# Decode attention with an MLP beside it: TensorE's attention work as one loop of four passes, with separate buffers for K and V

## The chip, the cores and the metric

The kernel runs on one core of a Trainium2 chip. The metric is the device time of one execution in microseconds (us), as the median of several runs. Times inside an execution come from one profiled run and are counted from the start of its span. TensorE is written PE, VectorE DVE, ScalarE ACT, GpSimd POOL, and SyncE, which issues nearly all DMAs here, SP. The core's DMA work is spread over 16 DMA engines.

## The reference

One token `x` of 1024 elements is normalised. Branch A is attention over a long cache: 32 query heads, 4 KV heads (8 query heads share one), 65,536 cached positions of 128 elements. Branch B is a small MLP with two residual steps. The weights and the two caches are bfloat16; K and V are 64 MiB each, and everything that is read is 169.87 MB.

```python
x = A_x; xn = layernorm(x)
# A: q = xn @ wq; for each of 4 KV heads, 8 query heads:
scores = einsum("bhqd,bhkd->bhqk", q, k) * Dh ** -0.5
o = einsum("bhqk,bhkd->bhqd", softmax(scores), v)
a = o.reshape(1, 1, 4096) @ wo
# B, on xn: h = gelu(layernorm(xn) @ w1) is shifted along the sequence
# and multiplied by w2; with one token every shifted part is zero, so x1 = xn
b = x1 + gelu(layernorm(x1) @ w3) @ w4
out = x + a + b
```

## The kernel before, in words

**Prologue.** `wq` (8 MiB), `w1`, `w2` (2 MiB each) and `w3` (7 MiB) are read into a large tile `KV` of three slots, 64 KiB in each partition, 8 MiB in all per slot. q is computed and spread into the tile `Yall` (L369), and branch B is computed up to the vector `gh_bf`, which is later multiplied by `w4`.

**Attention.** The cache is worked through in 8 blocks m (two for each KV head h) of 32,768 positions; the K part and the V part of a block are one slot each (8 MiB, one DMA of 128 rows of 64 KiB). A load i is K of block (i-3)/2 for odd i and V for even i. Slots rotate: `slot(i)` is i mod 3 (L278). So K and V share three buffers. `issue(i)` (L281) puts a load on SP's queue, where it waits until the slot's last readers and writers are done. V of block m+1 is issued after `QK(n+3)` of block m (L584), since its slot is the one that held K of block m; K of block m+2 is issued after the last `PV` of block m (L605), since its slot held V of block m. The first loads and the last stand outside this pattern: K of block 0 is issued behind the q projection, V of block 0 behind the use of `w2`, K of block 1 behind the end of the prologue; `wo` takes the place of the load behind the last K, and `w4` follows in four pieces (L532).

A block has four sub-blocks n to n+3, and their work is written out by hand in one order for all engines (L557 to L605). Each engine executes its own part of this order, in order. The pieces:

- `Ttr` (L436): DVE transposes K in place, 32x32 blocks, as float32 pairs of bfloat16. A sub-block takes four instructions of 128x1024. They are interleaved with the small DVE steps below: the pieces of sub-block n+2 and n+3 stand between `MAX`, `EXP` and `PTr`.
- `QK` (L448): 16 matmuls against `Yall` of the head, into the PSUM bank `S_ps[n % 4]`.
- `MAX` (L455 to L458): a maximum over two banks on DVE, a small product `Rm` on DVE, a matmul on PE that brings the groups together in `M_ps`.
- `EXP` (L465 to L476): on DVE the running minimum `brun` of the negated maxima; on ACT the exponentials `p_sb` of two sub-blocks with their sums; the factor `ff` by which older sums are scaled.
- `PT` and `PTr` (L479, L483): a permuting matmul into the one bank `PT_ps`, then a DVE transpose into `pT_f`.
- `PV` (L492): 16 matmuls of `pT_f` with V into `OT_ps`.
- `FLUSH` (L500 to L505): two sub-blocks' result is added to `O_acc`; at a head's first, ACT copies it.
- `combine_1` and `combine_2` (L509 to L527): a head's sum is inverted, and its four rows of output are brought into the columns of `o_bf`. For head h-1 they stand in the first block of head h, behind `QK(n)` and behind `QK(n+1)`; for the last head behind the loop.

**Output.** `out_resid` (L552), the 32 rows of `o_bf` times `wo`, and the 28 rows of `gh_bf` times `w4` (L543) accumulate in one PSUM bank; a copy (L612) and a DMA (L613) bring the result out.

**Synchronisation.** A small planner in Python records for each engine a list of waits and operations. Each engine has one semaphore that counts its finished operations (`_Q`, `c_pe`, `c_dve`, ...), each DMA channel another. For each buffer `_deps` (L73) adds a wait for each semaphore that wrote or reads it, unless the same engine has waited for as high a value of that semaphore before. PE also waits on its own semaphore. PE's whole program, prologue, eight blocks and output, is written out as straight code of some 3,340 records in the trace (1,627 weight loads, 1,611 matmuls, 98 semaphore instructions and a drain).

The order of one block before:

```python
Ttr(n, range(4)); QK(n)
Ttr(n + 1, range(4)); QK(n + 1)
Ttr(n + 2, [0, 1]); MAX(2 * m); Ttr(n + 2, [2]); EXP(2 * m); Ttr(n + 2, [3])
QK(n + 2); PT(n); Ttr(n + 3, [0]); PTr(n)
PT(n + 1); Ttr(n + 3, [1]); PTr(n + 1); Ttr(n + 3, [2, 3])
PV(n); QK(n + 3); issue(6 + 2 * m)
PV(n + 1); MAX(2 * m + 1); EXP(2 * m + 1); FLUSH(2 * m)
PT(n + 2); PTr(n + 2); PT(n + 3); PTr(n + 3)
PV(n + 2); PV(n + 3); FLUSH(2 * m + 1); issue(7 + 2 * m)
```

Of the kernel before, what the change touches and what calls it, by code (L numbers as in the profile page):

```python
# [13 lines left out]
class _Q:  # L14
    def __init__(self, name, sem):
        self.name = name
        self.sem = sem
        self.ops = []
        self.cnt = 0
        self.waited = {}  # L20

    def wait(self, ev):
        if ev is None:
            return
        sem, val = ev
        if self.waited.get(sem, 0) >= val:
            return
        self.waited[sem] = val
        self.ops.append((0, sem, val))

    def op(self, fn, tick=True):
        if tick:
            self.cnt += 1
            self.ops.append((1, fn, True))
            return (self.sem, self.cnt)
        self.ops.append((1, fn, False))
        return None

    def dma(self, fn, sem, val):
        self.ops.append((2, fn, sem))  # L40
        return (sem, val)

    def emit(self, eng):
        for o in self.ops:
            if o[0] == 0:
                eng.wait_ge(o[1], o[2])
            elif o[0] == 1:
                ins = o[1](eng)
                if o[2]:
                    ins.then_inc(self.sem, 1)  # L50
            else:
                o[1](eng).then_inc(o[2], 16)
# [20 lines left out]
def _deps(q, reads, writes):  # L73
    for b in reads:
        for s, v in b.w.items():
            q.wait((s, v))
    for b in writes:
        for s, v in b.w.items():
            q.wait((s, v))
        for s, v in b.r.items():  # L80
            q.wait((s, v))
# [12 lines left out]
def _op(q, fn, reads=(), writes=(), partial=False):  # L94
    _deps(q, reads, writes)
    ev = q.op(fn, True)
    _done(ev, reads, writes, partial)
    return ev
# [25 lines left out]
def bass_parallel_sum__gqa_block_cached__mixer_s_mlp__decode_kernel(  # L124
# [31 lines left out]
    with ExitStack() as es:  # L156
# [18 lines left out]
        Yall = sb("Yall", [P, HKV, 4, 4, G], BF)  # L175
        p_sb = sb("p_sb", [P, 2, 512], BF)
# [64 lines left out]

        q_pe = _Q("pe", sem("c_pe"))
        q_dve = _Q("dve", sem("c_dve"))
        q_act = _Q("act", sem("c_act"))
# [10 lines left out]
        b_x = _B(); b_xT = _B(); b_xn = _B(); b_xn2 = _B(); b_qT = _B(); b_Y = _B()  # L255
        b_ln = _B(); b_misc = _B(); b_h1 = _B(); b_x1 = _B(); b_xn3 = _B(); b_gh = _B(); b_acc = _B()
        b_KV = [[_B() for _ in range(16)] for _ in range(3)]
# [4 lines left out]
        b_Oacc = _B(); b_L = _B(); b_cb = _B(); b_o = _B(); b_orow = _B()  # L262
# [9 lines left out]
        b_w1 = b_KV[1][0:4]  # L272
        b_w2 = b_KV[1][4:8]
# [4 lines left out]
        def slot(i):  # L278
            return i % 3

        def issue(i):  # L281
            if i < 3 + 2 * NBLK:
                m, isv = divmod(i - 3, 2)
                h, nb = divmod(m, BPH)
                cache = A_v_cache if isv else A_k_cache
                src = cache[0, h, nb * BLK:(nb + 1) * BLK, :].rearrange("(p c) d -> p (c d)", p=P)
                kv_load(slot(i), "s%d" % slot(i), src, SLOT)
# [5 lines left out]
        q_pool.wait(evs[-1])  # L293
# [7 lines left out]
        q_pool.wait(ev)  # L301
# [7 lines left out]
        q_pool.wait(ev)  # L309
# [114 lines left out]
        for q in (q_pe, q_dve, q_act, q_pool):  # L424
            q_sp.wait((q.sem, q.cnt))
# [5 lines left out]
        def Ttr(n, idx):  # L431
            m, sub = divmod(n, 4)
            s = slot(3 + 2 * m)
            for ix in idx:
                o = 4096 * sub + 1024 * ix
                _op(q_dve, lambda e, o=o: e.transpose(out=KV32[:, s, o:o + 1024], in_=KV32[:, s, o:o + 1024]),  # L436
                    reads=[b_KV[s][4 * sub + ix]], writes=[b_KV[s][4 * sub + ix]])

        def QK(n):
            m, sub = divmod(n, 4)  # L440
            h = m // BPH
            s = slot(3 + 2 * m)
            fns = []
            for we in range(4):
                w_hi, e_ = divmod(we, 2)
                for cm in range(4):
                    mv = bass.AP(KV[:].tensor, s * SLOT + sub * 8192 + cm * 128 + w_hi * 64 + e_, [[kvstep, P], [512, 16], [2, 32]])
                    fns.append(lambda e, we=we, cm=cm, mv=mv: e.matmul(  # L448
                        S_ps[32 * cm:32 * cm + 32, n % 4, :], Yall[:, h, we, :, :].rearrange("p a g -> p (a g)"), mv,
                        start=(we == 0), stop=(we == 3), tile_position=(0, 32 * cm)))  # L450
            _grp(q_pe, fns, reads=b_KV[s][4 * sub:4 * sub + 4] + [b_Y], writes=[b_S[n % 4]])

        def MAX(g):
# [3 lines left out]
                reads=[b_mrow[k], b_const], writes=[b_R[k]])  # L457
# [3 lines left out]
        def EXP(g):  # L461
# [4 lines left out]
            else:  # L466
# [5 lines left out]
                reads=b_S[2 * k:2 * k + 2] + [b_brun[k]], writes=b_p + [b_lp[k]])  # L472
# [9 lines left out]
        def PTr(n):  # L482
            _op(q_dve, lambda e: e.transpose(out=pT_f[:, n % 2, :], in_=PT_ps[:, :]), reads=[b_PT], writes=[b_pT[n % 2]])  # L483

        def PV(n):
# [9 lines left out]
            _grp(q_pe, fns, reads=[b_pT[n % 2]] + b_KV[s][4 * sub:4 * sub + 4], writes=[b_OT[g % 2]], partial=(last == 1))  # L495

        def FLUSH(g):
            k = g % 2
            if g % (2 * BPH) == 0:
                _op(q_act, lambda e: e.activation(O_acc[:, 0:512], OT_ps[:, k, :], ACTF.Copy), reads=[b_OT[k]], writes=[b_Oacc])  # L500
                _op(q_dve, lambda e: e.tensor_copy(O_acc[:, 512:513], lp[:, k:k + 1]), reads=[b_lp[k]], writes=[b_L])
                return
            _op(q_dve, lambda e: e.scalar_tensor_tensor(out=O_acc[:, 512:513], in0=O_acc[:, 512:513], scalar=ff[:, k:k + 1], in1=lp[:, k:k + 1], op0=ALU.mult, op1=ALU.add),
                reads=[b_ff[k], b_lp[k], b_L], writes=[b_L])
            _op(q_dve, lambda e: e.scalar_tensor_tensor(out=O_acc[:, 0:512], in0=O_acc[:, 0:512], scalar=ff[:, k:k + 1], in1=OT_ps[:, k, :], op0=ALU.mult, op1=ALU.add),  # L505
                reads=[b_ff[k], b_OT[k], b_Oacc], writes=[b_Oacc])

        def combine_1(h):
            _op(q_pe, lambda e: e.matmul(M_ps[:, 32:33], Dmat_f[:, :], O_acc[:, 512:513], start=True, stop=True),  # L509
                reads=[b_L, b_const], writes=[b_M])  # L510
            _op(q_dve, lambda e: e.reciprocal(cb_rL[:, :], M_ps[:, 32:33]), reads=[b_M], writes=[b_cb])
            _op(q_dve, lambda e: e.tensor_scalar(out=cb_W[:, :, :, :].rearrange("p t g i -> p (t g) i"),
                                                 in0=maskT[:, :, :].rearrange("p t g -> p (t g)").unsqueeze(2).broadcast_to([P, 4 * G, 4]), scalar1=cb_rL[:, 0:1], scalar2=None, op0=ALU.mult),
                reads=[b_cb, b_const], writes=[b_cb])

        def combine_2(h):
            r0 = 32 * h
            fns = []
            for t in range(4):
                fns.append(lambda e, t=t: e.matmul(M_ps[r0:r0 + 32, 128:256], cb_W[:, t, :, :].rearrange("p g i -> p (g i)"), O_acc[:, t * P:(t + 1) * P],  # L520
                                                   start=(t == 0), stop=(t == 3), tile_position=(0, r0)))
            _grp(q_pe, fns, reads=[b_Oacc, b_cb], writes=[b_M])
            _op(q_dve, lambda e: e.tensor_tensor(out=cb_R[r0:r0 + 32, :].rearrange("p (a j) -> p a j", j=32), in0=M_ps[r0:r0 + 32, 128:256].rearrange("p (a j) -> p a j", j=32),  # L523
                                                 in1=maskD[r0:r0 + 32, :].unsqueeze(2).broadcast_to([32, 4, 32]), op=ALU.mult),
                reads=[b_M, b_const], writes=[b_cb])
            _op(q_dve, lambda e: e.reduce_sum(cb_o[r0:r0 + 32, :], cb_R[r0:r0 + 32, :].rearrange("p (a j) -> p j a", j=32), axis=AX.X), reads=[b_cb], writes=[b_cb])
            _op(q_dve, lambda e: e.tensor_copy(o_bf[r0:r0 + 32, :], cb_o[r0:r0 + 32, :]), reads=[b_cb], writes=[b_o], partial=True)  # L527
# [4 lines left out]
        def w4_dma(i):  # L532
            r0, nr = w4_parts[i]
            _dma(q_sp, chan("w4%d" % i), lambda e: e.dma_start(out=KV[:, slot(20), r0 * D:(r0 + nr) * D], in_=rows_src(B_w4, r0, nr)), writes=[b_W4[i]])
# [21 lines left out]

        for m in range(NBLK):  # L557
            n = 4 * m
            h, nb = divmod(m, BPH)
            comb = nb == 0 and h > 0  # L560
            Ttr(n, range(4))
            QK(n)
            if comb:
                combine_1(h - 1)
            Ttr(n + 1, range(4))
            QK(n + 1)
            if comb:
                combine_2(h - 1)
            Ttr(n + 2, [0, 1])
            MAX(2 * m)  # L570
            Ttr(n + 2, [2])
            EXP(2 * m)
            Ttr(n + 2, [3])
            QK(n + 2)
            PT(n)
            Ttr(n + 3, [0])
            PTr(n)
            PT(n + 1)
            Ttr(n + 3, [1])
            PTr(n + 1)  # L580
            Ttr(n + 3, [2, 3])
            PV(n)
            QK(n + 3)
            issue(6 + 2 * m)  # L584
            if m == NBLK - 1:
                for i in range(len(w4_parts)):
                    for bk in b_KV[slot(20)]:
# [13 lines left out]
            FLUSH(2 * m + 1)  # L601
            if m == NBLK - 2:
                kv_load(slot(19), "s%d" % slot(19), A_wo.rearrange("(p r) n -> p (r n)", p=P), SLOT)
            else:
                issue(7 + 2 * m)  # L605
        out_resid()
        combine_1(HKV - 1)
        combine_2(HKV - 1)
        out_rows([(o_bf[:, j:j + 1], KV[:, slot(19), j * D:(j + 1) * D]) for j in range(32)], b_KV[slot(19)] + [b_o])
        for i, (r0, nr) in enumerate(w4_parts):  # L610
            out_rows([(gh_bf[:, r:r + 1], KV[:, slot(20), r * D:(r + 1) * D]) for r in range(r0, r0 + nr)], [b_W4[i], b_gh], last=(i == len(w4_parts) - 1))
        _op(q_dve, lambda e: e.tensor_copy(orow[:, :], OUT), reads=[b_OUT], writes=[b_orow])  # L612
        ev_out = _dma(q_sp, chan("out"), lambda e: e.dma_start(out=out[0, 0, :].rearrange("(j n) -> j n", j=4), in_=orow[0:97:32, :]), reads=[b_orow])  # L613
        q_sp.wait(ev_out)
# [13 lines left out]
        q_pe.emit(nc.tensor)  # L628
# [28 lines left out]
```

## Time and profile before

| what | value |
|---|---|
| median of 8 runs | 402.06 us (401.66 to 402.37) |
| the profiled execution's own time | 402.11 us |
| its span, first to last instruction | 400.9 us |
| read from HBM | 169.87 MB, 424 GB/s over the span |
| PE, DVE, ACT, POOL busy | 178.6, 224.6, 25.2, 7.1 us |
| granted TensorE clock, mean | 0.623 |
| loads of K issued (block 2, 3, 4) | 105.83, 142.75, 188.12 us |
| loads of V issued (block 1, 2, 3) | 96.44, 133.27, 179.37 us |
| first transpose of block 0, 1, 2, 3 | 71.7, 108.14, 146.89, 188.7 us |

The span is the time from the first to the last instruction that the profiler recorded; the execution's own time is 1.2 us longer. The page divides the span into 40 slices and gives for each the busy tenths of every engine and the DMA engines' mean share. A timeline lists an engine's instructions with start, duration, and in square brackets the idle time before one and what released it. An answer by stages gives for stretches of time the busy time of each engine, the granted PE clock, and, as the last two columns, the share of 16 DMA engines and the rate of the packets that began in that stretch; a packet of 64 KiB counts with its whole duration in the stretch in which it begins, so short stretches can show more than 1.

### The profile page before, as it was taken

Reading aid. Unit: us, or ns where it says so; the run is one execution under the profiler, and the core shown is the slowest. Engines: PE = TensorE matmul, PEld = TensorE weight load, DVE = VectorE, ACT = ScalarE, POOL = GpSimd, SP = SyncE. Lnnn points to the kernel's source line nnn. Section 1 sums busy time; section 2 is a strip of 40 time slices with the busy share of each in tenths; the row PEclk is TensorE's granted clock in tenths of the full one; section 3 lists DMA queues with packets and bytes.
Section 4 is the critical chain, followed back from the end, with each engine's and each line's share of the span. In section 5 each row is a group of like instructions: output and inputs, shape, how many; then the busy total and the mean of one; then the engine's idle time right before and its main releaser. Section 6 shows DMA issues by size and latency. Waiting matters only on the chain.

```text
span 400.9 us, 3966 instructions
## 1 busy us (share of the span) xinstructions
PE 178.6 (45%) x1611; PEld 71.3 (18%) x1627; DVE 224.6 (56%) x347; ACT 25.2 (6%) x53; POOL 7.1 (2%) x30
## 2 busy tenths in 40 slices
PE   0035669136434523374345242633462345437655
PEld 0022435011111101121111020111121111102332
DVE  0024230985498446764985548659746684696400
ACT  1000000011001100101011001000110011010100
POOL 5000000000000000000000000000000000000000
PEclk9998656555655565658556655575576655555785
DMA  9999999999999999999999999999999999999994
GB/s 419 419 391 486 387 465 451 425 420 425 425 425 459 445 425 425 414 445 426 453 438 425 414 419 451 433 439 438 414 432 419 452 438 427 432 440 432 395 419 192
DMA packets 3770, 170.13 MB, mean 424 GB/s; under 512 B 548, under 2 KB 552, under 8 KB 808
## 3 DMA queue, kind: packets, MB, share of 16 engines
q1 hardware_dynamic: 3608, 169.87, 98.4%
q8 instruction: 13, 0.21, 0.2%
q14 instruction: 5, 0.04, 0.0%
q10 hardware_dynamic: 144, 0.00, 0.0%
HBM read 169.87 MB, written 0.00 MB: 424 GB/s over the span
## 4 chain that ended last, share of the span: by engine, by line
DMA 41%; DVE 30%; PE 24%; issue 3%; another core or an unknown queue 2%; POOL 0%; SPq 0%; ACT 0%; DVEq 0%
DMA KV<-in_A_k_cache_dram 28%; DVE KV L436 21%; PE S_ps L448 8%; DMA KV<-in_B_w_dram 7%; DMA KV<-in_A_x_dram 6%; PE OT_ps L492 5%; PE S_ps L385 3%; DVE pT_f L483 2%; PE M_ps L400 2%; PE S_ps L353 2%; DVE mrow L455 2%; PE M_ps L520 1%; DVE Yall L369 1%; PE PT_ps L479 1%
## 5 line engine op out<-in xcount | busy, mean ns | idle before, releaser
L436 DVE STREAM_TRANSPOSE KV<-KV 128x1024 f32<-128x1024 f32 x128 | 148.6, 1211 | 7.5 <-DMA KV<-in_A_k_cache_dram 7.4
L448 PE MATMUL S_ps<-KV,Yall 128*32 128x512 bf16 x512 | 60.7, 622 | 113.1 <-DVE KV L436 113.1
L492 PE MATMUL OT_ps<-KV,pT_f 128*32 128x512 bf16 x512 | 58.4, 605 | 1.3 <-PE OT_ps L492 1.3
L448 PEld LDWEIGHTS S_ps<-KV,Yall 128*32 128x32 bf16 x512 | 16.7, 125 | 145.8 <-DVE KV L436 129.9
L483 DVE STREAM_TRANSPOSE pT_f<-PT_ps 128x512 f32<-128x512 f32 x32 | 22.6, 706 | 28.3 <-PE S_ps L448 12.0
L470 ACT ACTIVATE p_sb<-S_ps,brun 128x1024 bf16<-128x1024 f32 x16 | 17.8, 1113 | 279.4 <-DVE brun L468 174.7
L455 DVE TENSOR_REDUCE mrow<-S_ps 128x1 f32<-128x1024 f32 x16 | 19.5, 1216 | 16.8 <-PE S_ps L448 16.7
L479 PE MATMUL PT_ps<-p_sb,permR 128*128 128x512 bf16 x16 | 9.0, 560 | 37.2 <-DVE pT_f L483 37.2
L492 PEld LDWEIGHTS OT_ps<-KV,pT_f 128*32 128x32 bf16 x512 | 17.0, 131 | 34.9 <-issue 33.1
L505 DVE SCALAR_TENSOR_TENSOR O_acc<-O_acc,ff,OT_ps 128x512 f32<-128x512 f32 x12 | 8.9, 746 | 22.4 <-PE OT_ps L492 22.4
L385 PE MATMUL S_ps<-KV 128*32 128x512 bf16 x88 | 12.5, 569 | 2.9 <-DVE KV L333 2.9
L458 PE MATMUL M_ps<-Rm,Lmat 128*128 128x16 bf16 x16 | 3.1, 192 | 22.3 <-DVE Rm L456 22.3
L313 DVE CAST KV<-KV 128x8 f32<-128x8 bf16 x1 | 0.2, 172 | 22.3 <-DMA KV<-in_A_x_dram 22.3
L479 PEld LDWEIGHTS PT_ps<-p_sb,permR 128*128 128x128 bf16 x32 | 3.3, 102 | 43.1 <-ACT p_sb L470 15.4
L612 DVE CAST orow<-S_ps 128x256 bf16<-128x256 f32 x1 | 0.4, 424 | 16.9 <-PE S_ps L543 16.9
L400 PE MATMUL M_ps<-ident_f,pT_f 64*128 64x2 f32 (+2 forms) x32 | 7.9, 373 | 2.3 <-DVE pT_f L393 2.3
L400 PEld LDWEIGHTS M_ps<-ident_f,pT_f 64*128 64x128 f32 (+2 forms) x32 | 7.7, 326 | 4.7 <-DVE pT_f L393 4.7
L393 DVE COPY pT_f<-S_ps 64x512 f32<-64x512 f32 (+1 forms) x3 | 2.1, 686 | 11.4 <-PE S_ps L385 11.4
L543 PE MATMUL S_ps<-KV,gh_bf 128*1 128x256 bf16 x112 | 5.6, 362 | 5.8 <-DMA KV<-in_B_w_dram 5.6
L523 DVE TENSOR_TENSOR cb_R<-M_ps,maskD 32x128 f32<-32x128 f32 x4 | 1.2, 288 | 12.1 <-PE M_ps L520 12.1
L458 PEld LDWEIGHTS M_ps<-Rm,Lmat 128*128 128x128 bf16 x16 | 1.6, 102 | 34.5 <-DVE Rm L456 34.5
L338 PE MATMUL M_ps<-KV 8*128 8x8 bf16 x1 | 0.2, 161 | 16.2 <-DVE Dmat_f L337 16.2
(82 smaller groups left out, 97.3 us busy)
## 6 DMA issues: line engine op xcount, KB each, us to landing
KV<-in_B_w_dram SPq DMA_DIRECT2D x1, 7168.0 KB, 48.0
KV<-in_B_w_dram SPq DMA_DIRECT2D x1, 4352.0 KB, 21.6
KV<-in_B_w_dram SPq DMA_DIRECT2D x2, 2048.0 KB, 28.3
KV<-in_B_w_dram SPq DMA_DIRECT2D x1, 1792.0 KB, 25.6
KV<-in_B_w_dram SPq DMA_DIRECT2D x1, 768.0 KB, 27.0
KV<-in_B_w_dram SPq DMA_DIRECT2D x1, 256.0 KB, 27.2
KV<-in_A_k_cache_dram SPq DMA_DIRECT2D x8, 38.8
KV<-in_A_v_cache_dram SPq DMA_DIRECT2D x8, 30.1
```

Source lines behind the costliest of these rows:

```text
L353: fns.append(lambda e, j=j, b=b, jj=jj: e.matmul(S_ps[32 * jj:32 * jj + 32, b, :], xn_bf[:, j:j + 1].broadcast_to([P, 32]), KV[:, 0, j * H ...
L385: fns.append(lambda e, j=j, k=k, mv=mv: e.matmul(S_ps[32 * (k % 4):32 * (k % 4) + 32, bank + k // 4, :], vec[:, j:j + 1].broadcast_to([P, ...
L400: fns.append(lambda e, b=b, nb=nb, c=c: e.matmul(M_ps[:, c0 + 16 * b + c:c0 + 16 * b + 4 * nb:4], pT_f[0:32 * nb, b, c:512:4], ident_f[0:3 ...
L436: _op(q_dve, lambda e, o=o: e.transpose(out=KV32[:, s, o:o + 1024], in_=KV32[:, s, o:o + 1024]), reads=[b_KV[s][4 * sub + ix]], writes=[b_ ...
L448: fns.append(lambda e, we=we, cm=cm, mv=mv: e.matmul(S_ps[32 * cm:32 * cm + 32, n % 4, :], Yall[:, h, we, :, :].rearrange("p a g -> p (a g ...
L455: _op(q_dve, lambda e: e.reduce_max(mrow[:, k:k + 1], S_ps[:, 2 * k:2 * k + 2, :].rearrange("p b c -> p (b c)"), axis=AX.X), reads=b_S[2 * ...
L470: _op(q_act, lambda e: e.activation(p_sb[:, :, :].rearrange("p b c -> p (b c)"), S_ps[:, 2 * k:2 * k + 2, :].rearrange("p b c -> p (b c)") ...
L479: _op(q_pe, lambda e: e.matmul(PT_ps[:, :], permR[:, :], p_sb[:, n % 2, :], start=True, stop=True), reads=[b_p[n % 2], b_const], writes=[b ...
L483: _op(q_dve, lambda e: e.transpose(out=pT_f[:, n % 2, :], in_=PT_ps[:, :]), reads=[b_PT], writes=[b_pT[n % 2]])
L492: fns.append(lambda e, q=q, q4=q4: e.matmul(OT_ps[32 * q4:32 * q4 + 32, g % 2, :], pT_bf[:, n % 2, q, :, 1], KV[:, s, 8192 * sub + 512 * q ...
L505: _op(q_dve, lambda e: e.scalar_tensor_tensor(out=O_acc[:, 0:512], in0=O_acc[:, 0:512], scalar=ff[:, k:k + 1], in1=OT_ps[:, k, :], op0=ALU ...
L543: fns.append(lambda e, lhs=lhs, rhs=rhs, jj=jj: e.matmul(S_ps[32 * jj:32 * jj + 1, 0, 0:256], lhs, rhs[:, 256 * jj:256 * jj + 256], start= ...
```

## The change

PE's program for the eight blocks becomes one loop of four passes, a pass for each head (two blocks). With it come:

- Two new semaphores, `l_dve` and `l_act`, count those DVE and ACT operations that PE waits for, from zero in each pass. All loads of V use one channel, `v`. At the end of a pass PE waits until these three have reached the pass's total and subtracts it, then branches back.
- K is in slot 0 and slot 2 by turns, V always in slot 1. V of block m+1 can so be issued only after the last `PV` of block m: `issue(6 + 2 * m)` moves from behind `QK(n+3)` to behind `FLUSH(2m+1)`, directly ahead of `issue(7 + 2 * m)`. The `w4` loads stay behind `QK(n+3)` of the last block, into slot 2; `wo` goes into slot 0.
- `QK` reads a tile `Ycur`, into which DVE copies the head's part of `Yall` at the start of each pass (`YC`).
- A `Ttr` is one DVE instruction of 128x4096 in place of four of 128x1024, and is no longer interleaved with `MAX`, `EXP` and `PTr`: `Ttr(n+2)` stands whole ahead of `MAX`, `Ttr(n+3)` whole behind `PTr(n+1)`.
- `combine` stands in one piece at the end of its own head, ahead of the branch, and its matmuls write the partitions 0 to 31 of `M_ps`.
- A head's first `FLUSH` copies `O_acc` on DVE, not ACT; the other `FLUSH` does its large step first.
- The planner keeps for each event what was known when it was issued, and leaves out a wait that another wait implies; PE no longer waits on its own semaphore.

The new block (the diff of the loop, cut):

```diff
 def slot(i):
-    return i % 3
+    m, isv = divmod(i - 3, 2)
+    return 1 if isv else 2 * (m % 2)
...
-    comb = nb == 0 and h > 0
-    Ttr(n, range(4))
+    if nb == 0:
+        loop_sync(h)
+        q_pe.mark({q.loop_sem: q.count[q.loop_sem] for q in (q_dve, q_act)})
+        YC(h)
+    Ttr(n)
     QK(n)
-    if comb:
-        combine_1(h - 1)
-    Ttr(n + 1, range(4))
+    Ttr(n + 1)
     QK(n + 1)
-    if comb:
-        combine_2(h - 1)
-    Ttr(n + 2, [0, 1])
+    Ttr(n + 2)
     MAX(2 * m)
-    Ttr(n + 2, [2])
     EXP(2 * m)
-    Ttr(n + 2, [3])
     QK(n + 2)
     PT(n)
-    Ttr(n + 3, [0])
     PTr(n)
     PT(n + 1)
-    Ttr(n + 3, [1])
     PTr(n + 1)
-    Ttr(n + 3, [2, 3])
+    Ttr(n + 3)
     PV(n)
     QK(n + 3)
-    issue(6 + 2 * m)
...
     PV(n + 2)
     PV(n + 3)
     FLUSH(2 * m + 1)
+    issue(6 + 2 * m)
     if m == NBLK - 2:
-        kv_load(slot(19), "s%d" % slot(19), A_wo.rearrange("(p r) n -> p (r n)", p=P), SLOT)
+        kv_load(0, "wo", A_wo.rearrange("(p r) n -> p (r n)", p=P), SLOT)
     else:
         issue(7 + 2 * m)
+    if nb == BPH - 1:
+        combine(h)
```

The pieces that are called, and how PE's program is written out:

```diff
+def YC(h):
+    _op(q_dve, lambda e: e.tensor_copy(Ycur[:, :, :, :].rearrange("p w a g -> p (w a g)"), Yall[:, h, :, :, :].rearrange("p w a g -> p (w a g)")),
+        reads=[b_Y], writes=[b_Yc], loop=True)
...
+def Ttr(n):
+    m, sub = divmod(n, 4)
+    s = slot(3 + 2 * m)
+    o = 4096 * sub
+    _op(q_dve, lambda e: e.transpose(out=KV32[:, s, o:o + 4096], in_=KV32[:, s, o:o + 4096]), reads=[b_KV[s][sub]], writes=[b_KV[s][sub]], loop=True)
...
-q_pe.emit(nc.tensor)
+q_pe.emit(nc.tensor, q_pe.ops[:marks[0]])
+for s_, v in entry.items():
+    nc.tensor.wait_ge(s_, v)
+with nc.tensor.Fori(0, HKV):
+    for waits, o in zip(steps, work[0]):
+        for s_, v in waits.items():
+            nc.tensor.wait_ge(s_, v)
+        q_pe.emit(nc.tensor, [o])
+    for s_, v in totals.items():
+        nc.tensor.wait_ge(s_, v).then_inc(s_, -v)
+q_pe.emit(nc.tensor, q_pe.ops[marks[-1]:])
```

## The prediction, as put on record before the result

> **What bounds the kernel now.** I read the page's slices and DMA queues first. The DMA engines are busy in every slice but the last, and the data queue fills 98.4% of them: 169.87 MB is what the reference must read, so only idle DMA time, or DMA time spent on something else, can be won or lost.
>
> ```profile
> DMA  9999999999999999999999999999999999999994
> q1 hardware_dynamic: 3608, 169.87, 98.4%
> q8 instruction: 13, 0.21, 0.2%
> DMA 41%; DVE 30%; PE 24%; issue 3%; another core or an unknown queue 2%; POOL 0%; SPq 0%; ACT 0%; DVEq 0%
> L436 DVE STREAM_TRANSPOSE KV<-KV 128x1024 f32<-128x1024 f32 x128 | 148.6, 1211 | 7.5 <-DMA KV<-in_A_k_cache_dram 7.4
> ```
>
> The chain (fourth line) ends in DMA or passes through DVE and PE, but this is one chain of several that are equally long: where it runs through DVE, the queue of loads is still full. Next SP's timeline, with each load's issue, and DVE's, with the wait for K of block 2:
>
> ```profile
> 96.44 0.33 SPq L265 DMA_DIRECT2D KV<-in_A_v_cache_dram  x1
> 105.83 0.33 SPq L265 DMA_DIRECT2D KV<-in_A_k_cache_dram  x1
> 133.27 0.33 SPq L265 DMA_DIRECT2D KV<-in_A_v_cache_dram  x1
> 142.75 0.33 SPq L265 DMA_DIRECT2D KV<-in_A_k_cache_dram  x1
> ...
> 146.89 2.37 DVE L436 STREAM_TRANSPOSE KV<-KV 128x1024 f32<-128x1024 f32 x2 [3.45 <-DMA KV<-in_A_k_cache_dram]
> ```
>
> V of block 2, issued at 133.27, is in the queue 13.6 us before K of block 2 has landed (146.89). That lead keeps the engines fed. Last, the stages at both ends (last two columns: DMA share and rate of packets that began there):
>
> ```profile
> 0.50:1.00 0.50, 0.00 (x0) 0.00 (x0) 0.00 (x0) 0.10 (x1) 0.09 (x1) 1.00 0.00 0
> 1.00:1.50 0.50, 0.00 (x0) 0.00 (x0) 0.00 (x0) 0.50 (x1) 0.50 (x5) 1.00 5.08 1704
> ...
> 394.00:395.00 1.00, 0.00 (x0) 0.00 (x0) 0.00 (x0) 0.00 (x0) 0.00 (x0) 0.50 0.69 279
> 395.00:396.00 1.00, 0.59 (x13) 0.38 (x17) 0.00 (x0) 0.00 (x0) 0.00 (x0) 0.50 0.62 236
> 396.00:397.00 1.00, 1.00 (x20) 0.41 (x12) 0.00 (x0) 0.00 (x0) 0.00 (x0) 0.50 0.31 123
> 397.00:398.00 1.00, 0.76 (x16) 0.24 (x12) 0.00 (x0) 0.00 (x0) 0.00 (x0) 0.50 0.09 33
> ```
>
> An idle engine starts 1.0 to 1.6 us after an issue. At the end the share fades over 3 us: the 16 engines don't finish together. The trace's landing records give each engine's share of a load: K of block 1 lands between 106.20 and 108.12, the last piece of `w4` between 394.40 and 397.92. A 64 KB packet takes 2.42 us, eight of them per engine and load 19.37 us, a pair of loads 38.74 us. The spread comes from packets that aren't data: each of the 13 instruction packets of the page occupies one engine for 1.02 to 1.11 us (13 times 1.0 is the page's 0.2%), and the data packet beside it takes 2.9 us, so that engine is 1.55 us later for good. They come each time PE has executed some 256 instructions (3,337 records, 13 packets). The latest engine, with two such delays and small ones, is 3.5 us behind the earliest, and it sets the end: 397.92 to 400.9 is the last rows, the copy and the output DMA, 3.0 us.
>
> **The change, part by part.**
>
> *Length of a block, from its first transpose to its last `PV`, call it L.* Before, blocks without a combine (0, 1, 3, 5, 7) take 34.1, 34.6, 33.7, 33.8, 33.6: mean 34.0; K is transposed at +22.8 (108.14 to 130.94). A merged `Ttr` isn't in the trace. Four pieces take 4.62 (ceiling); one piece of 1.20 plus 3072 elements at the slope between L483 (512 elements, 0.71) and L436 (1024, 1.21), 0.97 ns, is 4.18 (floor); I take 4.4. The new order: three `Ttr` 13.2; `MAX` and `Rm` 1.4 (to 14.6); from `Rm`'s start to the minimum 0.56, `brun` 0.2, ACT 0.33 later (15.5). PE does `QK(n+2)` behind the small matmul, at 15.0; 2.47 from there to `PTr` as in block 1, 1.49 to the next, 0.7 its length: 19.65. The last `Ttr` ends at 24.05. So what the interleaving hid, waits of DVE for PE and ACT, is now open, against shorter transposes: +1.25 (0.4 to 2.1 by the two ends). L is 35.25. PE's waits on itself (0.17 us ahead of four groups in a block at most) give back some 0.25: 35.0. `YC` costs 0.2 (a small copy, L413, takes 0.19); `FLUSH` on DVE 0.75 beside ACT's exponentials; both small.
>
> *Combine.* It no longer stops DVE twice inside the next block (blocks 2 and 4 took 41.2 and 41.6, 7 us more than the others), but stands between heads: `FLUSH` 1.0, sum matmul 0.6, reciprocal and weights 0.5, four float32 products 1.9, three DVE steps 0.9, with handovers 5.1 us, with `YC` 5.3 from the last `PV` to the next transpose. Within a head that gap is 1.0. A head costs 2 x 35.0 + 6.3 = 76.3 against 77.5 of pure DMA: it fits, barely.
>
> *V's single buffer.* V of block m+1 now comes at the end of block m. Block 0 starts at 71.9 (the prologue stays) and ends at 107.0. Before, V of block 1 was issued at 96.44 and its packets began as K of block 1 left the engines, from 106. Now the engines run dry: restart 1.0 to 1.6 after 107.0, and first packets in an empty system took 2.7 to 3.4, not 2.42 (the first loads: all done by 4.3 us after issue). That is as if all began at 107.0 + 1.9 = 108.9. The earliest engine loses 2.8 us, the latest (108.12) only 0.8. Later blocks start with K's landing, so their end, 35.0 later, leaves 3.7 us until the next K, against 1.9 for a restart; behind a combine 2 us less, and early engines may wait, but not the latest. The second buffer for K costs nothing.
>
> *The end.* `wo` and `w4` are issued in the old order behind V of block 7, two loads ahead of need. Block 7 starts with its K (before, at 344.6, behind a late block 6; after, near 346), so its last `PV` and the last combine are over by 386, its rows with `wo` (5.3 us before) by 392; the first piece of `w4` landed at 391.06 before and moves with the DMA time to about 394. Covered. The waits left out on DVE, ACT and SP are semaphore instructions on engines that idle: nothing.
>
> *PE's loop.* Wait and decrement at the pass's end find their counts reached: nothing. The body is some 583 records (3,337 less 439 ahead of the attention and 565 behind it, by four), 2.3 pages of 256. No jump is in this trace. Either the pages are kept (nothing more is fetched), or a jump fetches some again, up to the whole program once more (1,590 instructions, 6 to 7 pages on as many engines) at each of three jumps. PE's own wait is covered: its part of the combine ends about 4.3 us behind the last `PV`, the next `QK` is due at 9.7, and another 2.3 may pass before `MAX` is late; so 7.7 us. The nearest row is straight code: a page for 256 instructions, two delays on the latest engine behind 108. I take that.
>
> [...]
>
> *Sum, for the latest engine.* 108.9 + 288.2 (earliest engine, 106.20 to 394.40) + 2 x 1.55 = 400.2; plus 3.0 of tail, 403.2 of span, against 400.9; plus 1.2 outside the span (402.11 less 400.9), **404.4 us**. The profiled run stands 0.05 above the median.
>
> **The rivals.**
>
> 1. *Forecast, 0.45:* block 0's gap, page delays as before. One to three delays and L within 1 us: 402.7 to 406.5.
> 2. *Each jump brings in much of the program again, 0.20:* three more delays on the same engines: 404.4 + 4.65 = 409.1; with two pages doubled, 407. For it: packets come in whole pages, ahead of use. Against it: nothing shows how many pages are kept.
> 3. *The block's length decides, 0.13:* if L exceeds 36 us or a jump takes over 8 us, a head costs more than 78.5, and the engines wait in every head. At L = 37 it is 80.3: 3 heads x 2.8 above 77.5, 8 us less the 3.1 of page delays that then lie in the waits: 409. For it: the spare of 1.2 us; against it: before, L varied by 1 us only.
> 4. *Fewer pages, 0.20, the other side:* if the loop's pages stay in PE's instruction memory, they are fetched once. With the gap and one delay 402.9, with none 401.3; if block 0 also ends by 105 (L = 33.2) only one delay is left on the earliest engines: 394.4 + 1.55 + 3.0 + 1.2 = 400.2. It turns to faster below one delay, or where the gap is under 1 us.
> 5. *The code isn't reached or the loop costs nothing and nothing else changes, 0.02:* 402.
>
> **How the numbers follow.** 0.2% of 402.06 is 0.8 us, about what can be told from no change here. Faster (under 401.3): 0.12, from rival 4. Same: 0.12, from rivals 4 and 5 and the lower edge of the forecast. Slower: 0.76. The range, 401.0 to 409.5, leaves out a tenth on each side; the forecast's own is 402.7 to 406.5.
>
> **What would show it.** In the changed profile: SP's timeline with V of block 1 issued near 107, and a DMA share of nearly 0 for 1 to 2 us behind 106; no such hole later. `Ttr` with a mean of 4.2 to 4.6. DVE idle inside blocks, at `PTr`. The page's instruction packets: 13 for the forecast, over 25 for rival 2, under 9 for rival 4. Last `PV` to next transpose 5.3 between heads. I am wrong if holes in the DMA share come in every head, if L is off by more than 1 us, or if PE is late at a pass's first `QK`.

## The result and the profile after

The changed kernel takes 404.33 us (median of 14 runs, 401.75 to 406.28); the kernel before takes 402.00 us beside it (40 runs, 401.66 to 402.54). The ratio is 1.0056, 95% interval 1.0045 to 1.0068: slower, as forecast, and within 0.1 us of the forecast time. (Ratios here and below are of the means of the runs, without the profiled one, so they differ a little from the quotient of the medians.) The runs also lie further apart: over 4.5 us, where those of before lie within 0.9. The profiled execution took 404.85 us, with a span of 403.6.

The page of the kernel after has these lines against those of before: the DMA share, the data and the instruction queue, the chain, the transposes.

```profile
DMA  9999999999999999999999999999999999999994
q1 hardware_dynamic: 3608, 169.87, 98.3%
q8 instruction: 6, 0.10, 0.1%
DMA 55%; DVE 25%; PE 17%; issue 1%; another core or an unknown queue 1%; SPq 0%; POOL 0%; ACT 0%
L460 DVE STREAM_TRANSPOSE KV<-KV 128x4096 f32<-128x4096 f32 x32 | 140.0, 4412 | 13.5 <-DMA KV<-in_A_k_cache_dram 13.5
```

The first two lines hardly moved, and that is the trap of this profile: the same 3,608 data packets fill 98.3% of a span that is 2.7 us longer. A packet counts as busy for its whole duration, so engines that work slowly look as busy as before (behind 106, below: share 1.29 against 0.99 for the same 426 GB/s). The third line is a gain: 6 instruction packets where there were 13. In the fourth line the chain runs through DMA for 55% of the span (41% before), and the last shows DVE waiting for K more than before (13.5 us against 7.5).

SP's timeline around block 0's end, and DVE's wait behind it:

```profile
104.01 0.33 SPq L290 DMA_DIRECT2D KV<-in_A_v_cache_dram  x1
104.38 0.43 SPq L290 DMA_DIRECT2D KV<-in_A_k_cache_dram  x1
...
108.17 4.45 DVE L460 STREAM_TRANSPOSE KV<-KV 128x4096 f32<-128x4096 f32 x1 [3.19 <-DMA KV<-in_A_k_cache_dram]
```

V of block 1 is issued only 4.2 us before K of block 1 has landed on all engines; before, it was 11.7 us (96.44 to 108.14). The landing and packet records of the trace, engine by engine, show what that does. Per block: when V of the next block is issued, when the first engine is done with K, the lead between the two, and how long V then takes on the latest engine (from K's last landing to V's last), where 19.37 us is the undisturbed time:

| end of block | V issued | K done, first engine | lead | V on the latest engine |
|---|---|---|---|---|
| 0 | 104.01 | 106.21 | 2.2 | 19.37 + 0.92 |
| 1 | 142.81 | 145.49 | 2.7 | 19.37 + 0.00 |
| 2 | 182.00 | 184.20 | 2.2 | 19.37 + 0.60 |
| 3 | 221.18 | 223.37 | 2.2 | 19.37 + 0.58 |
| 4 | 260.50 | 262.69 | 2.2 | 19.37 + 0.10 |
| 5 | 299.81 | 301.85 | 2.0 | 19.37 + 0.21 |
| 6 | 339.07 | 341.25 | 2.2 | 19.37 + 0.44 |

The sum is 2.85 us. The engines hardly stand idle (some 11 engine-us in all up to 394, of some 6,200); V's first packets are slow, on some engines the second ones, 2.7 to 4.1 us where a packet takes 2.42. Without those of the very first load, 63 packets take over 0.3 us too long up to 380 us, and together they lose 44 engine-us; before it was 16 packets, ten of them directly behind an instruction packet. By stages behind block 0's end (last two columns: DMA share and GB/s of the packets begun there), first after, then before:

```profile
106.00:108.00 2.00, 0.00 (x0) 0.00 (x0) 0.00 (x0) 0.00 (x0) 0.00 (x0) 0.68 1.29 426
108.00:110.00 2.00, 0.00 (x0) 0.00 (x0) 1.83 (x1) 0.00 (x0) 0.00 (x0) 0.50 0.85 328
```

```profile
106.00:108.00 2.00, 0.00 (x0) 0.00 (x0) 0.52 (x1) 0.00 (x0) 0.00 (x0) 1.00 0.99 426
108.00:110.00 2.00, 0.00 (x0) 0.00 (x0) 1.86 (x2) 0.00 (x0) 0.00 (x0) 0.72 1.14 492
```

After the change as many packets begin in the first stage, but they last longer (share 1.29 against 0.99), and fewer follow. The latest engine's sum is 108.15 + 288.2 (what the earliest engine took before, from 106.20 to 394.40) + 2.85 + some 1.5 for an instruction packet in the tail = 400.7; the last landing was at 400.86. That packet begins at 386.92, takes 0.99, and the data packet behind it takes 1.80 in place of 1.29. Before, the last landing was at 397.92.

The loop itself costs PE nothing that shows. DVE's and PE's timeline behind the first branch back:

```profile
147.83 8.76 DVE L460 STREAM_TRANSPOSE KV<-KV 128x4096 f32<-128x4096 f32 x2
...
152.32 0.14 PEld L474 LDWEIGHTS S_ps<-KV,Ycur 128*32 128x32 bf16 x8 [5.88 <-DVE KV L460]
152.32 1.90 PE L474 MATMUL S_ps<-KV,Ycur 128*32 128x512 bf16 x16 [5.43 <-DVE KV L460]
```

The second pass's first `QK` starts about 0.1 us behind its transpose, and what it waited for was DVE, not its own instructions. Instruction packets (the page's q8, 16 KB each) came at 43.6, 79.2, 106.0 and 145.7, then none until 386.9: the second to fourth pass fetched nothing. At the start of the third and the fourth pass the first `QK` also begins 0.1 us behind its transpose (at 230.81 and 309.45).

### The profile page after: what moved, and what is told of

It reads as the page before. It is cut to its first block, busy times and chain, and to the rows that moved or that the text cites. A ratio compares the mean times of both kernels' runs of the same rounds, so it can differ in the third digit from the quotient of the medians.

```text
span 403.6 us, 3656 instructions
## 1 busy us (share of the span) xinstructions
PE 178.7 (44%) x1611; PEld 68.0 (17%) x1627; DVE 222.8 (55%) x259; ACT 23.3 (6%) x49; POOL 7.1 (2%) x30
## 3 DMA queue, kind: packets, MB, share of 16 engines
q1 hardware_dynamic: 3608, 169.87, 98.3%
## 4 chain that ended last, share of the span: by engine, by line
DMA 55%; DVE 25%; PE 17%; issue 1%; another core or an unknown queue 1%; SPq 0%; POOL 0%; ACT 0%
DMA KV<-in_A_k_cache_dram 42%; DVE KV L460 17%; DMA KV<-in_B_w_dram 8%; DMA KV<-in_A_x_dram 5%; PE S_ps L474 4%; PE OT_ps L518 4%; PE S_ps L411 3%; DVE pT_f L509 2%; PE M_ps L426 2%; PE S_ps L379 1%; DVE mrow L481 1%; PE PT_ps L505 1%; DVE Yall L395 1%; DVE pT_f L419 1%
## 5 line engine op out<-in xcount | busy, mean ns | idle before, releaser
L460 DVE STREAM_TRANSPOSE KV<-KV 128x4096 f32<-128x4096 f32 x32 | 140.0, 4412 | 13.5 <-DMA KV<-in_A_k_cache_dram 13.5
L474 PE MATMUL S_ps<-KV,Ycur 128*32 128x512 bf16 x512 | 60.7, 623 | 95.3 <-DVE KV L460 95.3
L474 PEld LDWEIGHTS S_ps<-KV,Ycur 128*32 128x32 bf16 x512 | 14.3, 125 | 132.1 <-DVE KV L460 114.5
L543 PE MATMUL M_ps<-O_acc,cb_W 128*32 128x128 f32 x32 | 6.9, 386 | 2.3 <-DVE cb_W L538 2.3
```

The source lines that it names most:

```text
L460: _op(q_dve, lambda e: e.transpose(out=KV32[:, s, o:o + 4096], in_=KV32[:, s, o:o + 4096]), reads=[b_KV[s][sub]], writes=[b_KV[s][sub]], l ...
L474: fns.append(lambda e, we=we, cm=cm, mv=mv: e.matmul(S_ps[32 * cm:32 * cm + 32, n % 4, :], Ycur[:, we, :, :].rearrange("p a g -> p (a g)") ...
L543: fns.append(lambda e, t=t: e.matmul(M_ps[0:32, 128:256], cb_W[:, t, :, :].rearrange("p g i -> p (g i)"), O_acc[:, t * P:(t + 1) * P], sta ...
```

## The experiments

Two groups were run, each beside the kernel before on the same chip (402.03 us for e1 to e4, 402.13 for e5 to e7). Theory A is that V's late issue makes its first packets slow; B blames the branch and the waits around it; C the longer blocks. A lead is, as above, the time from V's issue to the first engine's landing of the K before it.

| kernel | us (range; runs) | ratio to before, interval | instruction packets | slow packets |
|---|---|---|---|---|
| before | 402.00 (401.66 to 402.54; 40) | 1 | 13 | 16 |
| changed | 404.33 (401.75 to 406.28; 14) | 1.0056 (1.0045 to 1.0068) | 6 | 63 |
| e1 no branch | 404.89 (403.53 to 406.53; 4) | 1.0081 (1.0051 to 1.0110) | 13 | 47 |
| e2 V in halves | 401.17 (400.97 to 401.45; 11) | 0.9979 (0.9970 to 0.9988) | 6 | 6 |
| e3 halves, no branch | 402.55 (402.37 to 403.22; 11) | 1.0014 (1.0005 to 1.0023) | 13 | 12 |
| e4 V and K later | 406.43 (403.89 to 407.32; 4) | 1.0088 (1.0060 to 1.0116) | 6 | 83 |
| e5 V as 3/4 and 1/4 | 401.27 (401.05 to 401.61; 10) | 0.9980 (0.9970 to 0.9989) | 6 | 9 |
| e6 K apart from V | 403.30 (401.96 to 404.92; 10) | 1.0025 (1.0008 to 1.0043) | 6 | 67 |
| e7 before, whole transposes | 403.08 (402.26 to 403.87; 10) | 1.0020 (1.0010 to 1.0029) | 13 | 20 |

Instruction packets are those of the trace's records for the queue q8, taken as PE's (13 with PE's straight code, 6 with the loop, 13 again in e1), one or two of which can lie behind the span's end; slow packets are those of 16 KB and more that took over 0.3 us longer than their size takes undisturbed, up to 380 us, without those of the very first load.

**e1: the changed kernel without the branch.**

```diff
-with nc.tensor.Fori(0, HKV):
+for _ in range(HKV):
```

The body stands four times in PE's program; waits and decrements stay.

> Theory A (V is issued too late: some 2.2 us ahead of the first engine's end of K, so that the first packets of V are slow in nearly every block; the loop itself saves instruction packets): the slow packets stay, the instruction packets come back to about 13, so 405 to 407 us. Rival B (the branch back and the waits at the end of a pass cost the time): without them about 402 us. Rival C (longer blocks from whole transposes): nothing changes, 404.3.

404.89, no faster than with the branch: B, which had about 402, falls. The instruction packets are back, in the page's third part:

```profile
q8 instruction: 13, 0.21, 0.2%
```

The time is just under the 405 to 407 that A gave, and from the changed kernel's 404.33 the four runs can't be told apart. That part of an instruction packet's delay is lost here in the early engines' wait for V is a guess that no run tests; e3, with 12 slow packets in place of 47, shows its cost better.

**e2: V in two halves, the first one issued earlier.**

```diff
+for hf in halves:
+    lo, hi = hf * SLOT // 2, (hf + 1) * SLOT // 2
+    _dma(q_sp, chan("v%d" % hf), ... out=KV[:, 1, lo:hi], in_=src[:, lo:hi], writes=b_KV[1][2 * hf:2 * hf + 2])
...
 PV(n + 1)
+issue(6 + 2 * m, (0,))
...
 FLUSH(2 * m + 1)
-issue(6 + 2 * m)
+issue(6 + 2 * m, (1,))
```

> The loop stays; V is loaded in two halves with a semaphore each, and the first half is issued behind the block's second PV, some 8 us earlier. Theory A: no packet of V takes over 2.6 us, instruction packets stay at 6, so 400.5 to 402.0 us and all runs within 1 us of each other (now 401.75 to 406.28). Rival B: the branch is still there, 404 us. Rival C: the blocks are as long as before, 404 us.

401.17, 0.21% under the kernel before, and all eleven runs within 0.5 us. The order of the work, the single buffer for V, the loop and the whole transposes are those of the changed kernel, and the blocks are about as long (34.1 us on average, 34.2 in the changed kernel, each from the first transpose to the last `PV`); half a load comes earlier, and V's packets are of 32 KB. (e5 speaks of the size.) SP's timeline at block 0's end (the first line is both halves, issued at 98.41 and 105.29; the duration is from the first to the end of the second):

```profile
98.41 7.21 SPq L316 DMA_DIRECT2D KV<-in_A_v_cache_dram  x2
105.66 0.43 SPq L290 DMA_DIRECT2D KV<-in_A_k_cache_dram  x1
```

The lead is 8.0 us (first engine done with K at 106.40), and 6 slow packets are left, of which 4 stand directly behind an instruction packet. Against C this is the plain test: blocks as long as in the changed kernel, and the loss is gone. The halves cost a little: a pair of loads takes the first engine 38.81 us (145.20 to 184.01) where it took 38.72 in the kernel before (144.92 to 183.64), 0.7 us over eight blocks. The last landings were between 395.21 and 397.22, before between 394.40 and 397.92: the earliest engine is later by that, the latest engine, which counts, earlier.

**e3: halves, without the branch.** Both edits.

> V in halves, and PE's program written out without the branch: 13 instruction packets, no late V. Theory A: what the instruction packets cost by themselves, 0.5 to 2 us above the same kernel with the loop, so 401.5 to 403 us. Rival B: faster than the same kernel with the loop. If the packets cost nothing, no difference.

402.55. With no late V in either, the kernel with the branch is faster by 1.38 us, so the instruction packets do cost, about one delay of the latest engine: in the profiled executions the last landing is at 398.70 here and 397.22 in e2, 1.48 us apart, and the prediction's price for one packet was 1.55. The page's own line:

```profile
q8 instruction: 12, 0.20, 0.2%
```

**e4: V and K issued still later.**

```diff
+q_sp.wait_all([_op(q_dve, lambda e: e.tensor_copy(late[:, 0:1], maskD[:, 0:1]), reads=[b_const], writes=[b_late])])
 issue(6 + 2 * m)
```

> The changed kernel with V and K issued another 1.1 us later, behind a small DVE copy that stands behind FLUSH. Theory A: V comes 1.1 us ahead of the first engine's end, more packets are slow and engines run dry for about 1 us in every block, 406 to 410 us. Rivals B and C: a millionth of the queue's work is moved, so 404.3 us.

406.43, 83 slow packets, and now engines that really stand idle: some 31 engine-us. (The four runs lie wide, and their interval overlaps that of the changed kernel, so the rise is less sure than the idle time.) By stages (last two columns: DMA share and GB/s of packets begun there), around block 0's end, where V was issued at 106.29, behind the first engine's end at 106.24:

```profile
106.00:108.00 2.00, 0.00 (x0) 0.00 (x0) 0.26 (x3) 0.00 (x0) 0.00 (x0) 1.00 1.60 533
108.00:110.00 2.00, 0.00 (x0) 0.00 (x0) 1.39 (x1) 0.00 (x0) 0.00 (x0) 0.54 0.00 0
110.00:112.00 2.00, 0.00 (x0) 0.00 (x0) 2.00 (x1) 0.00 (x0) 0.00 (x0) 0.50 1.21 524
```

All sixteen engines start this V between 107.2 and 107.8, thirteen of them after standing idle for 0.3 to 2.0 us, and finish its first packets only behind 110: no packet begins between 108 and 110. They all finish this V within 0.6 us of each other (127.48 to 128.10): here the wait went first to the engines that were ahead. Nor did every block lose: at the ends of blocks 1 and 5 the lead was 3.1 and 3.4 us, since K had come later, and no packet of V was slow there; the latest engine lost most at the ends of blocks 4 and 6 (1.6 and 2.1 us), with leads of 1.9 and 1.1.

**e5: three quarters of V behind the third `PV`, one quarter behind the fourth.**

```diff
+lo, hi = ((0, 3 * SLOT // 4), (3 * SLOT // 4, SLOT))[hf]
...
 PV(n + 2)
+issue(6 + 2 * m, (0,))
 PV(n + 3)
```

> The loop stays; three quarters of V are issued behind the block's third PV, 1.4 to 1.9 us ahead of its end, the last quarter behind the fourth. Theory A with a threshold just above 2.2 us (block 1 of the changed kernel had 2.7 us and hardly a slow packet): a lead of about 4 us is enough, no slow packets, 401 to 402 us. If a new load needs much more than 4 us to run at full speed: 403 to 404.5 us.

401.27, the same as e2 within the intervals. The lead is 2.5 us at block 0, where three packets of V are still slow, and 3.3 to 4.4 later, where one is that doesn't stand behind an instruction packet (at 264.5). So the smaller packets (48 KB here) aren't what helps: at the short lead they are slow too. The kernel before, with a lead of 3.0 at the end of block 4 (258.04 to 261.07), has two slow packets there (3.16 and 2.83 us), and its latest engine loses nothing by them. So in these runs some 3 us of lead were enough, and 2.2 were not: about 1 to 2 us of earlier issue decided about 3 us of time.

**e6: K of block m+2 issued apart from V.**

```diff
 Ttr(n)
 QK(n)
+if m > 0:
+    q_sp.wait_all([(q_pe.sem, q_pe.cnt)])
+    ...
+    issue(5 + 2 * m)
...
-    issue(7 + 2 * m)
```

> The changed kernel, but K of block m+2 is issued some 9 us behind V, after the first QK of the next block, still 12 us ahead of the end of V. If the first packets of V are slow because V comes late: 404.3 us as before, slow packets in most blocks. If they are slow because the descriptors of two loads are written at the same time: the slow packets go, 401 to 402.5 us.

The slow packets stay (67 against 63), and their lost time too (44 engine-us in both profiles): they don't come from two loads being issued 0.4 us apart. But the median is 403.30, 1 us under the changed kernel's and between the two forecasts; the two medians come from different groups, both kernels' runs lie 3 us and more apart, and no count in the profiles explains the microsecond. Whether the two issues cost a part of the time stays open.

**e7: the kernel before, with whole transposes in the new order.**

```diff
-for ix in idx:
-    o = 4096 * sub + 1024 * ix
-    _op(q_dve, ... KV32[:, s, o:o + 1024] ...)
+o = 4096 * sub
+_op(q_dve, ... KV32[:, s, o:o + 4096] ...)
```

> The kernel before, with only the transposes changed: one of 128x4096 for four of 128x1024, in the new order. Theory A: blocks 0.3 to 1.3 us longer, hidden under a queue of loads that is never short: 402.0 us, within 0.2%. Rival C (block length decides): 403 us or more.

403.08, 0.2% above before, its interval just clear of 1: more than A allowed (402.8), and just what C gave (403 or more). So A as forecast here missed. In the kernel before, combines lie inside blocks 2, 4 and 6, ahead of V's issue, and these leads are the shortest (4.3, 3.0 and 4.0 us, against 7.7 to 11.7 at the other ends); whole transposes take more of them. SP's timeline at the end of block 6, first of e7, then of the kernel before:

```profile
337.35 0.33 SPq L265 DMA_DIRECT2D KV<-in_A_v_cache_dram  x1
```

```profile
334.47 0.33 SPq L265 DMA_DIRECT2D KV<-in_A_v_cache_dram  x1
```

The first engine is done with K of block 7 at 338.50 in both (338.51 before). The lead falls from 4.0 to 1.15 us, and the slow packets that e7 has beyond those beside instruction packets stand there (six of 2.87 to 3.22 us that begin between 338.3 and 341.0). So the longer blocks used up the lead. That this is what costs the time isn't shown: those packets make V 0.7 us later on the earliest engine and 0.1 on the latest. In the profiled execution, the slowest of the ten, the last landing is at 399.49, 1.57 us later than before, and up to the first piece of `w4` only 0.18 of that is there (391.24 against 391.06). The rest comes from an instruction packet at 393.39 that falls on an engine that is late already. Where the time goes in the other runs is open. That block length isn't what slows the changed kernel rests on e2.

## Why the prediction was right, and where it wasn't

The sign, the size and the range came out right; two terms of the sum were wrong in opposite ways.

- **What bounds the kernel, and which engine counts.** Right. In all nine profiles the span ends 2.5 to 3.0 us behind the latest DMA engine's last landing, and the 1.55 us for an instruction packet was confirmed by e3 against e2 (1.48).
- **V's single buffer: place right, size and spread wrong.** The prediction had 0.8 us on the latest engine at block 0 and nothing later ("early engines may wait, but not the latest"). That step failed: the loss came back in five of the six later ends of blocks, 2.85 us in all. Two things were missed. The lead of 3.7 us was counted from K's landing on the latest engine, but the first engine is up to 2.5 us ahead of that, so its lead was 2.2 even with blocks shorter than forecast. And a restart wasn't only a wait of the engines that ran dry: at block 0's end the three engines that began V last, 3.3 to 3.5 us behind its issue, also had slow first packets (2.94 to 3.85 us). The 4.3 us for the first loads was short too: the last of their sixteen first packets ended 4.78 us behind the issue. Rival 3's picture, a loss in every head, was nearer, but by the queue, not by blocks that no longer fit.
- **Length of a block.** Predicted 35.0 on average, measured 34.3 (33.8 to 34.6, up to V's issue). `Ttr` was exact (4.41 against 4.4). PE gave back more than was allowed for: the two `PV` behind each other take 3.6 us, where before they took 4.0 at the same granted clock (0.50, between 138 and 143 us in both). The dropped waits on itself are the likely cause; no run tests them alone. The prologue ended 1.5 us earlier in this execution; over the profiles of all nine kernels it ends between 69.9 and 71.9, so that is no merit of the change. So V of block 1 was issued at 104.01, not 107.0, and the hole of 1 to 2 us behind 106 that the prediction named did not appear; slow packets stood in its place.
- **Combine.** 5.0 us from the last `PV` to the next transpose (142.81 to 147.83), predicted 5.3. At the three ends of heads the next transpose begins 0.0, 0.5 and 0.9 us behind K's landing (147.80, 225.85, 304.02).
- **PE's loop.** The forecast took 13 instruction packets and two delays, 3.1 us. Measured are 6 packets and one delay of some 1.5 on the latest engine, as in rival 4, to which 0.20 was given: a body of some 583 records, 2.3 times the 256 of a packet, was branched back to three times with no packet between 145.7 and 386.9 and without a late `QK`. What a longer body would do, no run shows.
- **The sum.** 0.8 + 3.1 = 3.9 us predicted above the undisturbed course, 2.85 + 1.5 = 4.4 measured; the tail was 0.3 shorter. The nearness to the median is luck to that extent: 2 us too little in one term, 1.6 too much in the other. And which engine an instruction packet falls on counts: of the 3.6 us between the last landings of the changed kernel and of e2, 2.1 are there when `wo` has landed (382.14 against 380.05), and 1.5 are the packet at 386.92, which falls on the latest engine here and not in e2. What the prediction didn't say is how far the runs would spread. That a lead so near its limit lets each run fall differently is likely, not shown; e2 and e5, clear of it, are as steady as the kernel before.

Rival 2 (pages read again at each branch) is excluded by the 6 packets, rival 5 by the time.

## What to carry to other kernels

In a kernel that DMA bounds, as here, a full DMA row isn't enough (98.3%, in a span 2.7 us longer): for each load compare its issue with the moment at which the *first* DMA engine runs out of the load before it. Here some 3 us between them were enough. A buffer can be given up if its load is cut in pieces that follow its readers, as e2 and e5 show: the loop then gains 0.2% over the kernel before, and the changed kernel loses 0.6% with the same buffers. Instruction packets were part of the DMA work here, and the loop, whose later passes fetched nothing, took more than half of them away (13 packets before, 6 after; between e3 and e2, 13 against 6, that was 1.38 us).

## What the runs showed of the hardware

- A load issued 2.0 to 2.2 us ahead of need ran its first packets at 2.7 to 4.1 us in place of 2.42, with some 11 engine-us of idle time in the whole execution; at 2.7 us of lead one block end went without loss on the latest engine, and at 3.0 to 4.4 us none lost time there by V's first packets (kernel before, e4, e5). The first loads' packets began 1.02 to 1.64 us after the first issue before and 1.01 to 1.75 after the change, those of e4's V at block 0's end 0.9 to 1.5 us after its issue; a lead of 2.2 us, longer than these, still gave slow first packets.
- One instruction packet of 16 KB delayed its DMA engine by about 1.5 us (changed kernel, packet at 386.92: 0.99 and 0.51 more for the data packet behind it; last landings of e3 and e2: 1.48 apart). In this kernel, which splits each load evenly over 16 engines, the engines ended apart: the last landings before lie between 394.40 and 397.92.
- PE fetched one instruction packet for each 256 instructions or so of straight code (13 for some 3,340), and none for the second to fourth pass of a loop of 583.
